# Attention and a linear-attention branch in one kernel: the four query chunks of a head group taken one after the other, with the order of the work written anew

## The chip, the cores and the metric

The kernel runs on one core of one Trainium2 chip. The metric is the device time of one execution in microseconds (us). The core has a matrix engine (PE), a vector engine (DVE), a scalar engine for activations (ACT), a general engine (POOL) and a queue for transfers (SP). They run side by side and wait for one another through semaphores.

## The reference, cut to what matters

The input x has 2048 tokens of 512 values. Two branches of 32 heads of 16 values each are computed from it and mixed by a gate per token.

```python
def _A_ref(x, wqkv, wo):                      # softmax attention
    q, k, v = ...                             # 32 heads of 16
    scores = jnp.einsum("bhqd,bhkd->bhqk", q, k) * (Dh ** -0.5)
    p = _softmax(scores, axis=-1)
    o = jnp.einsum("bhqk,bhkd->bhqd", p, v)
    return ... @ wo
def _B_ref(x, wqkv, w_phi, wo):               # linear attention
    phi_q = concat(softmax(q @ w_phi), softmax(-(q @ w_phi)))   # the same for k
    kv = einsum(phi_k, v); z = sum(phi_k)
    o = (phi_q @ kv) / (phi_q @ z + 1e-6)
    return ... @ wo
g = _sigmoid((x * gate_w).sum(-1, keepdims=True))
return g * a + (1 - g) * b
```

Branch A needs 32 x 2048 x 2048 exponentials, which is most of the work.

## The kernel before, in words

**Tiles of branch A.** The 2048 queries are cut into four chunks of 512 (`qc` 0 to 3), the 32 heads into four groups of eight (`cp` 0 to 3). A *step* is one pair (qc, cp). `ORDER` lists the 16 steps. Each step has two halves of four heads, so there are 32 half steps. A half step goes through the 16 tiles of 128 keys; one such tile for four heads is a *pack* (512 packs in all), and a pack has four *units*, one for each head: 128 keys by 512 queries, held as a 128x512 tile. There are 2048 units.

**Two ways for a unit.** Most units go through ACT: PE makes the scores in a ring of five PSUM banks (`_scores`, L1253), ACT takes the exponential of three and of two units in turn (`_exp`, L1304), and PE multiplies the result with the values (`_values`, L1378). Some packs are taken from ACT: `SHARES` says how many packs of each half step. Such a pack is a *batch* (`_vector_batch`): DVE copies each of its four score tiles out of PSUM with a scale (`v_bits`, L1155), and then four instructions over all four units (`v_line`, L1167) make four bit patterns, which read as bf16 numbers add up to the exponential. Bits of `POOLED` say which of the four lines of a batch run on POOL; the others run on DVE. PE then multiplies each pattern with the values, two of the four with values weighted by a constant. These weighted values lie in `VW` and are made on POOL by `v_scale` (L1131), four instructions each time `cp` differs from that of the step before.

**Projections.** Queries of a step are projected some 42 packs ahead (`_proj_q`, copied to `qraw`, moved by eight small transfers to `qT`). Keys and values are projected once for each group `cp` and each quarter j of the tokens (`_proj_k`, copied at L961; `_proj_v`, copied at L1041), and stay in `kT` and `V` to the end. Their due time is that of the group's first step plus `KAT + KSTEP*j` (values `VAT + VSTEP*j`), in packs. In the order of before each group is first met at step 0, 2, 4 and 6, so all keys and values are made in the first half.

**Normalising and output of A.** After each half step the sums are transposed, divided and scaled by the gate on DVE (`_norm`, `_normed`), and written to `onTA`, which has three buffers taken in turn by `qc`.

**Branch B.** Keys first (`_b_keys`, due at `K0 + SK*t` for token tile t), then queries in four blocks of four tiles (`_b_queries`, due at `Q0 + SQ*t`). Both go through `_b_soft`: a projection, a copy (L1548), a tree of maxima and differences on DVE, one exponential on ACT (L1585), a transposing transfer to `turns` (L1593), sums on PE and a scaling on DVE. Queries go on by a transposing transfer to `phiT` (L1671), to the product with the keys' sums, to `onB` (L1698), and by a transposing transfer to `onTB` (L1703). `onTB` has room for four token tiles, so a block's transfer waits until the block before has been read by the output.

**Output.** For each token tile eight matmuls, four from `onTB` (L1719) and four from `onTA` (L1763), then a copy on DVE (L1749) and a transfer out. `_out` puts a chunk's four tiles after its last step (`_done`), the last chunk's go through `_out_last` (L1791, L1801, L1804).

**The order.** The kernel writes out a fixed instruction order for each engine. `Plan.order` is a list scheduler that runs while the kernel is built: each operation has a cost, a due time (`prio`) and an earliest time (`rel`), in packs; it takes the operation that can start first, and among those the one that is due first. `NUDGE`, `HURRY`, `EASE`, `QEASE`, `LEASE` and `OEASE` are tables that shift single due times. Engines run their list in order, so one late operation holds all behind it. `PORT` names the operations which the scheduler never lets run on DVE and POOL at the same time: the lines, the scalings of `VW`, and the elementwise operations of branch B and the normalising among them; it writes a wait for that. When PE would have too little to do, it gets matmuls with zero weights (`_fill`, L1387).

Of the kernel before, what the change touches and what calls it, by code (L numbers as in the profile page):

```python
# [10 lines left out]
P = 128  # L11
# [58 lines left out]
class Plan:  # L70
# [10 lines left out]
    AHEAD, ENTER = 0.11, 0.011  # L81
# [310 lines left out]
class _Kernel:  # L392
# [6 lines left out]
    POOLED = (2, 15, 3, 10, 13, 12, 9, 14, 2, 6, 0, 7, 1, 13, 12, 3, 4, 11, 1, 1, 1, 13, 14, 0, 1, 0, 6, 10, 10, 2, 1, 3, 0, 1,  # L399
# [16 lines left out]
    OREL = 2  # L416
    ENDS = 10
    HURRY = (-10.7, 3.7, -1.9, -3.8, -1.4, 0.0, 0.0, 4.8, -2.6, -5.6, 17.9, 7.0, -7.0, 13.6, -1.6, 6.6, 2.3, 4.9, 15.5, 9.2,
# [5 lines left out]
    HASTE = 10  # L424
    QEASE = (0, 6.0, -7.0, 2.5, 3.8, 2.2, -6.3, -1.1, 0.2, -0.1, 6.2, -3.3, 0.0, 0.0, 0.4, -5.5)
    LEASE = (4.5, 6.9, -6.1, -1.6, 8.1, -2.7, 0, 0.0, 2.8, 1.7)
    OEASE = (0.3, 0, 0, 0, -0.6, 4.1, -0.7, 1.8, 5.0, 0, 3.4, 0, 0, 0, 0, 0)
    EASE = (14.0, -3.9, -11.6, 0.0, -2.6, 1.9, 2.0, 3.6, 4.6, -1.0, -0.8, -4.4, 6.4, 3.2, -1.7, 4.3, -1.2, -3.8, -1.2, 1.8,
# [5 lines left out]
    NUDGE = {  # L434
        'b_max': {1: 5.0, 2: 3.3, 3: -27.2, 4: 8.3, 6: -1.0, 7: 1.5, 8: -16.1, 10: -11.6, 13: 5.1, 14: -22.6, 16: -3.1,
# [5 lines left out]
        'b_mul': {1: -7.8, 4: 7.4, 5: -7.7, 7: -0.3, 8: 10.2, 9: 3.3, 10: 7.3},  # L441
        'b_ratio': {1: -4.3, 2: -18.2, 3: -0.7, 4: 2.1, 5: 5.9, 7: -0.2, 8: 18.9, 9: 3.5, 10: 7.2},
        'b_rec': {1: -6.3, 2: 3.4, 3: 5.3, 4: 23.1, 5: 0.9, 6: 14.6, 7: 0.9, 10: 1.4},
        'b_sum': {1: -4.9, 2: -2.5, 3: 1.1, 4: -8.4, 5: -1.9, 6: -4.7, 8: -18.1, 9: -18.6, 10: 3.4, 11: 2.3, 12: -30.0,
            13: -7.5, 14: -7.7, 15: 3.8, 18: 1.9, 19: 5.2, 20: -10.9, 21: 6.2, 23: -4.0, 24: -1.0, 25: -4.7, 26: 10.3,
            27: 9.6, 28: 2.4, 29: 9.6, 30: -23.7, 32: -0.3},
        'bn_den': {2: -10.7, 3: -2.5, 4: 5.5, 5: 4.0, 6: 9.9, 8: -11.3},
        'bn_mul': {2: -13.6, 3: 2.6, 4: -19.3, 5: -3.4, 6: 3.9, 7: -9.5, 8: -8.8, 9: 0.9, 11: -5.8, 12: 9.2, 13: 2.2,
            14: -0.5, 15: 3.7},
        'bn_rec': {1: 13.8, 2: -0.5, 4: -0.9},  # L450
# [5 lines left out]
        'bv_ev': {1: 24.2, 2: 11.4, 3: -6.4, 4: 3.4, 5: 1.7, 7: -6.7, 10: -8.6, 11: -23.4, 12: -3.9, 13: 4.1, 14: -4.1,  # L456
            15: -10.2},
        'den': {1: -23.3, 2: 16.1, 3: 5.2, 4: -4.6, 5: 9.8, 6: 8.6, 8: -20.2, 10: -3.7, 11: -10.3, 12: -3.5, 13: 5.0,
            14: -1.3, 16: -4.7, 18: 2.4, 19: 17.5, 20: 19.9, 21: -3.2, 23: -3.7, 24: -6.7, 25: -9.8, 26: -9.1, 29: -0.3,
            30: 10.3, 31: -0.4, 32: 6.9},  # L460
        'kproj': {1: 0.8, 3: 16.6, 4: 2.3, 5: -16.1, 6: 11.8, 9: -13.0, 10: 2.0, 11: 12.0, 12: 10.1, 13: -21.2, 14: -6.2,
# [808 lines left out]
    def _qk(self, a, b):  # L1270
# [582 lines left out]
```

## Time and profile before

| | |
|---|---|
| three timed runs | 779.84, 782.51, 783.31 us (median 782.51) |
| the profiled execution | 779.79 us, of which 778.0 us are the span of its instructions |
| ACT busy | 761.5 us of the span |
| PE, DVE, POOL busy | 746.7, 660.3, 337.3 us |
| batches taken from ACT | 110 of 512 packs (the sum of `SHARES`) |
| lines of these batches | 440, of them 160 on POOL |

An engine's busy time is the union of its instructions' times, so that instructions that overlap are not counted twice; the mean of one instruction is its whole duration. "Idle before" is the idle time of the engine in front of an instruction, with the instruction of the other engine that ended it. PE's busy time holds the zero matmuls too.

### The profile page before, as it was taken

The page shows a single profiled execution, that of the slowest core. Times are in us where ns is not written, and L with a number is a line of the kernel's source. Part 1 is how long each engine was busy: PE and PEld are TensorE (multiplying, and loading weights), DVE is VectorE, ACT ScalarE, POOL GpSimd, SP SyncE. Part 2 cuts the span into 40 slices and gives each one's busy share as a digit, 9 for nine tenths or more (in the row PEclk, how much of TensorE's full clock was granted, in tenths as well). Part 3 has the DMA queues.
Part 4 walks back from the last instruction along what each step waited for, and adds up shares of the span by engine and source line. Part 5 has one row for each costly group of instructions (what it writes and reads, how often), then busy time and mean ns, then how long its engine had stood idle before and what let it go on. Part 6 is the DMA issues. An engine that isn't in the chain of part 4 may idle for free.

```text
span 778.0 us, 20056 instructions
## 1 busy us (share of the span) xinstructions
PE 746.7 (96%) x8809; PEld 263.7 (34%) x8844; DVE 660.3 (85%) x1158; ACT 761.5 (98%) x658; POOL 337.3 (43%) x215
## 2 busy tenths in 40 slices
PE   8999999999999999999999999999999999999998
PEld 4333332333333333323333233322323333333345
DVE  5678887998889898888988898889897998888996
ACT  7999999999999999999999999999999999999997
POOL 4634254543432523554562423533435434354540
PEclk9999999999999999999999999999999999999999
DMA  9601110100304000003310033200024010331100
GB/s 240 198 5 35 28 30 7 29 8 2 63 1 63 1 2 8 2 1 63 69 22 28 3 59 64 37 21 5 5 43 75 2 22 15 62 56 29 28 3 31
DMA packets 82311, 28.44 MB, mean 37 GB/s; under 512 B 71984, under 2 KB 82224, under 8 KB 82224
## 3 DMA queue, kind: packets, MB, share of 16 engines
q1 hardware_dynamic: 81552, 26.97, 17.3%
q8 instruction: 69, 1.13, 0.6%
q10 hardware_dynamic: 672, 0.20, 0.1%
q14 instruction: 18, 0.15, 0.1%
HBM read 6.31 MB, written 2.10 MB: 11 GB/s over the span
## 4 chain that ended last, share of the span: by engine, by line
ACT 44%; PE 28%; DVE 19%; POOL 7%; issue 1%; DMA 1%; DVEq 0%
ACT ET L1304 43%; PE ps L1253 9%; PE ps L1378 7%; DVE blocks L1155 5%; DVE blocks L1167 5%; POOL blocks L1167 4%; PE ps L939 4%; PE ps L1387 3%; POOL over L1167 2%; DVE over L1167 2%; DVE over L1155 1%; DVE octs L1583 1%; ACT bq L1585 1%; PE ps L1035 1%; DMA turns<-bq 1%
## 5 line engine op out<-in xcount | busy, mean ns | idle before, releaser
L1304 ACT ACTIVATE ET<-ps 128x1536 bf16<-128x1536 f32 (+1 forms) x643 | 732.5, 1298 | 6.1 <-PE ps L1253 5.4
L1253 PE MATMUL ps<-qT,kT 32*128 32x512 bf16 (+2 forms) x2248 | 305.9, 364 | 12.1 <-ACT ET L1304 4.2
L1167 POOL TENSOR_SCALAR blocks<-blocks 128x2048 int16<-128x2048 f16 x85 | 161.3, 1897 | 167.7 <-DVE over L1167 64.6
L1155 DVE TENSOR_SCALAR blocks<-ps 128x512 f16<-128x512 f32 x316 | 207.2, 683 | 25.6 <-PE ps L1253 24.5
L1253 PEld LDWEIGHTS ps<-qT,kT 32*128 32x128 bf16 x2248 | 83.5, 91 | 248.7 <-ACT ET L1304 115.3
L1378 PE MATMUL ps<-ET,V 128*32 128x512 bf16 (+2 forms) x1772 | 146.3, 363 | 0.7 <-DVE over L1155 0.3
L1387 PE MATMUL ps<-kT,zero 128*32 128x512 bf16 (+1 forms) x1460 | 119.8, 384 | 0.0
L1167 DVE TENSOR_SCALAR blocks<-blocks 128x2048 int16<-128x2048 f16 x153 | 103.5, 687 | 11.8 <-POOL blocks L1167 6.2
L1155 DVE TENSOR_SCALAR over<-ps 128x512 f16<-128x512 f32 x124 | 81.6, 683 | 11.6 <-PE ps L1253 11.2
L1167 POOL TENSOR_SCALAR blocks<-over 128x2048 int16<-128x2048 f16 x27 | 51.2, 1897 | 91.5 <-DVE over L1167 31.5
L1167 POOL TENSOR_SCALAR over<-blocks 128x2048 int16<-128x2048 f16 x28 | 53.1, 1897 | 55.7 <-DVE blocks L1167 14.9
L1378 PE MATMUL ps<-blocks,VW 128*32 128x512 bf16 (+1 forms) x692 | 60.7, 365 | 1.7 <-DVE blocks L1167 1.0
L1378 PE MATMUL ps<-blocks,V 128*32 128x512 bf16 (+1 forms) x676 | 60.7, 368 | 1.6 <-DVE blocks L1167 0.6
L1378 PEld LDWEIGHTS ps<-ET,V 128*32 128x32 bf16 x1772 | 42.7, 96 | 48.6 <-issue 29.1
L1167 POOL TENSOR_SCALAR over<-over 128x2048 int16<-128x2048 f16 x20 | 37.9, 1897 | 42.2 <-DVE blocks L1167 22.3
L1131 POOL TENSOR_SCALAR VW<-V 128x544 bf16<-128x544 bf16 x40 | 25.7, 645 | 66.7 <-PE ps L1378 24.1
L1387 PEld LDWEIGHTS ps<-kT,zero 128*32 128x32 bf16 x1460 | 31.9, 94 | 53.8 <-issue 43.8
L939 PE MATMUL ps<-WB,xT 128*128 128x512 bf16 x169 | 45.8, 381 | 4.3 <-issue 2.3
L1167 DVE TENSOR_SCALAR blocks<-over 128x2048 int16<-128x2048 f16 x50 | 34.4, 688 | 5.4 <-PE ps L1253 2.8
L1167 DVE TENSOR_SCALAR over<-blocks 128x2048 int16<-128x2048 f16 x50 | 34.3, 687 | 5.0 <-POOL blocks L1167 3.5
L939 PE MATMUL ps<-xT,WA 128*128 128x512 bf16 (+1 forms) x124 | 35.7, 380 | 1.4 <-DVE blocks L1155 0.8
L1585 ACT ACTIVATE bq<-octs 128x4096 bf16<-128x4096 f16 (+1 forms) x10 | 29.8, 2979 | 0.0
(98 smaller groups left out, 533.6 us busy)
## 6 DMA issues: line engine op xcount, KB each, us to landing
qT<-qraw SPq DMA_DIRECT2D x120, 16.0 KB, 1.8
xn<-in_A_x_dram SPq DMA_DIRECT2D x3, 512.0 KB, 6.0
WB<-in_B_wqkv_dram SPq DMA_DIRECT2D x3, 512.0 KB, 5.2
out_dram<-WB SPq DMA_DIRECT2D x12, 128.0 KB, 1.7
WA<-in_A_wqkv_dram SPq DMA_DIRECT2D x3, 384.0 KB, 4.5
xn<-in_A_x_dram SPq DMA_DIRECT2D x2, 256.0 KB, 3.6
WoA<-in_A_wo_dram SPq DMA_DIRECT2D x1, 512.0 KB, 4.1
WoB<-in_B_wo_dram SPq DMA_DIRECT2D x1, 512.0 KB, 4.9
```

Of the source, the lines that this page charges most:

```text
L939: mm = op("PE", lambda e, c=c: e.matmul(self._bank(job)[:, 0:n], lhs(c), rhs(c), start=(c == 0), stop=(c == 3)), self.c_pe(n), reads=reads ...
L1035: ins = e.matmul(self._bank(job)[:, P * tt:P * tt + P], self.xT[:, 4 * j + tt, c], self.WA[:, 2, c, P * cp:P * cp + P], start=(c == 0), st ...
L1131: self.plan.op("POOL", lambda e, q=q: e.tensor_scalar(self.VW[:, q, 0:544].rearrange("p (t v) -> p t v", v=136), self.V[:, 4 * q:4 * q + 4 ...
L1155: parts.append(op("DVE", lambda e, j=j, job=job: e.tensor_scalar(x[:, j, :], self._bank(job), SCALE * LOG2E * 128, FLOOR, op0=ALU.mult, op ...
L1167: op("POOL" if pooled else "DVE", lambda e, tile=tile, line=line: e.tensor_scalar(flat(tile).bitcast(I16), flat(x), 1.0, line, op0=ALU.mul ...
L1253: ins = e.matmul(out[u][:, cols], self.kT[32 * i:32 * i + 32, cp, kt * TOK:(kt + 1) * TOK], self.qT[32 * i:32 * i + 32, s, q], start=True, ...
L1304: o = plan.op("ACT", lambda e: e.activation(self.ET[:, a % NS:a % NS + n, :], self.ps[:, a % NR:a % NR + n, :], ACT.Exp, scale=SCALE), sel ...
L1378: ins = e.matmul(self._bank(ot)[32 * i:32 * i + 32, to], values, tile[:, cols], start=first and j == 0, stop=ot.final[i] is op and j == le ...
L1387: ins = e.matmul(self._bank(ot)[32 * i:32 * i + 32, lo:QCH], self.zero[:], self.kT[:, 0, lo:QCH], start=False, stop=False, tile_position=( ...
L1583: return e.tensor_tensor(wide(signs(off_)[:, :, s_]), a, b, ALU.subtract)
L1585: made = [op("ACT", lambda e: e.activation(flat, off_, ACT.Exp), 0.03 + self.c_act(n), reads=b_half, name="b_exp", prio=due + 1, lat=0.53)]
```

## The change

The steps are taken in another order: all four chunks of group 0, then all four of group 1, and so on. With it:

- Keys and values of group `cp` are due from 96 (84) packs before the group's first step on, 24 packs apart, where it was 42 (36) and 12. As before, each is projected once.
- All four chunks are now finished in the last quarter, so `onTA` has four buffers. Room for that comes from `qraw` (one buffer for two), and from `wphi` and `iden`, which now share memory with `onB`. `phiT` lies over the first half of `kT` (groups 0 and 1), no longer over `WA`; its first transfer waits for the readers of these keys.
- The zero matmuls read `xT`, no longer `kT`.
- `v_scale` follows the change of group: at 4 of the 16 steps, where it was 10.
- Branch B is drawn out: keys due at 18 + 16t (was 18 + 9.5t), queries at 330 + 12t (was 216 + 17t).
- `SHARES` sums to 113 (was 110): by groups of eight half steps 28, 27, 34, 24, where it was 22, 29, 31, 28. Of the 452 lines 161 are marked for POOL (44, 34, 47, 36 by the same groups; before 43, 43, 40, 34).
- Every table of shifts is another one, and three constants of the scheduler (`AHEAD`, `OREL`, the latency of the transfer to `onTB`).

```diff
-    AHEAD, ENTER = 0.11, 0.011
+    AHEAD, ENTER = 0.07, 0.011
...
-    ORDER = ((0, 0), (1, 0), (0, 1), (1, 1), (0, 2), (1, 2), (0, 3), (1, 3),
-             (2, 0), (3, 0), (2, 1), (3, 1), (2, 2), (2, 3), (3, 2), (3, 3))
+    ORDER = tuple((qc, cp) for cp in range(4) for qc in range(4))
-    KAT, KSTEP, VAT, VSTEP = -42, 12, -36, 12
+    KAT, KSTEP, VAT, VSTEP = -96, 24, -84, 24
-    OREL = 2
+    OREL = 3
...
+        self.wphi = nc.alloc_sbuf_tensor_at("wphi", [P, 4, P], BF16, offset=onb_at)
+        self.iden = nc.alloc_sbuf_tensor_at("iden", [P, P], BF16, offset=onb_at + 1024)
+        self.qraw = sb("qraw", [P, 1, QCH], BF16)
+        self.onTA = sb("onTA", [P, 4, 4, QCH], BF16)
-        self.phiT = nc.alloc_sbuf_tensor_at("phiT", [P, 4, 8, TOK], BF16, offset=wa_at + 4 * D * 2)
+        self.phiT = nc.alloc_sbuf_tensor_at("phiT", [P, 4, 8, TOK], BF16, offset=kt_at)
...
-    SHARES = (1, 2, 3, 5, 2, 3, 4, 2, 3, 5, 3, 4, 3, 4, 3, 4, 4, 3, 4, 3, 4, 6, 3, 4, 3, 5, 3, 2, 4, 5, 3, 3)
+    SHARES = (2, 3, 3, 3, 4, 6, 2, 5, 2, 4, 3, 5, 3, 4, 2, 4, 5, 5, 4, 4, 3, 4, 3, 6, 1, 6, 1, 3, 3, 3, 3, 4)
...
-                e.matmul(self.ps[:, a % NR, :], self.kT[:, 0, 0:P], self.kT[:, 0, 0:QCH], start=True, stop=True)
+                e.matmul(self.ps[:, a % NR, :], self.xT[:, 1, 0], self.xT[:, 1].rearrange("p c q -> p (c q)"), start=True, stop=True)
...
-        dst, b_dst = self.onTA[:, qc % 3, g8 // 2, :], self.b_onTA[qc % 3][g8 // 2]
+        dst, b_dst = self.onTA[:, qc, g8 // 2, :], self.b_onTA[qc][g8 // 2]
...
-    K0, SK, Q0, SQ = 18.0, 9.5, 216.0, 17.0
+    K0, SK, Q0, SQ = 18.0, 16.0, 330.0, 12.0
...
+        if not self.b_early:
+            self.b_early = [*self.b_k0, *self.b_kT[0], *self.b_kT[1]]
+            for b in self.b_phiT:
+                b.readers = [r for x in self.b_early for r in x.readers]
...
-            reads=self.b_onB, writes=self.b_onTB[tt:tt + 2], prio=due + 2, lat=2.9)
+            reads=self.b_onB, writes=self.b_onTB[tt:tt + 2], prio=due + 2, lat=3.1)
```

More of the change, by code (lines that the diff above doesn't have):

```diff
@@ L678, in sb @@
             return t
-        self.iden = sb("iden", [P, P], BF16)
         self.mask = sb("mask", [P, 2], F32)
@@ L703, in _memory @@
         self.sides = sb("sides", [P, 2, 4], BF16)
+        kt_at = (at[0] + 63) // 64 * 64
         self.kT = sb("kT", [P, 4, S], BF16)
@@ L712, in _memory @@
         self.rB = sb("rB", [P, 2, H], F32)
+        onb_at = (at[0] + 63) // 64 * 64
         self.onB = sb("onB", [P, 2, D], BF16)
-        self.qraw = sb("qraw", [P, 2, QCH], BF16)
-        self.onTA = sb("onTA", [P, 3, 4, QCH], BF16)
+        self.wphi = nc.alloc_sbuf_tensor_at("wphi", [P, 4, P], BF16, offset=onb_at)
+        self.iden = nc.alloc_sbuf_tensor_at("iden", [P, P], BF16, offset=onb_at + 1024)
+        self.qraw = sb("qraw", [P, 1, QCH], BF16)
+        self.onTA = sb("onTA", [P, 4, 4, QCH], BF16)
         wt_at = (at[0] + 63) // 64 * 64
@@ L846, in _projections @@
         self.b_qraw = [B(), B()]
-        self.b_onTA = [[B() for _ in range(4)] for _ in range(3)]
+        self.b_onTA = [[B() for _ in range(4)] for _ in range(4)]
         self.b_T1 = [B(), B()]
@@ L1015, in _proj_q @@
         reads = [self.b_xT[qc], self.b_WA[0][cp > 0], self.b_mask]
-        raw = self.qraw[:, n % 2]
+        raw = self.qraw[:, 0]
         self._proj(lhs, rhs, reads, [lambda e, b: e.tensor_copy(raw, b)], self.c_dve(512), due, due - 10, "qproj",
-                   [self.b_qraw[n % 2]])
+                   [self.b_qraw[0]])
         parts = [lambda e, i=i, side=side: e.dma_start(
@@ L1021, in _proj_q @@
             raw[32 * i + 16 * side:32 * i + 16 * side + 16, :]) for side in range(2) for i in range(4)]
-        o = self.plan.op("SP", parts, 0.63 * len(parts), reads=[self.b_qraw[n % 2]], writes=[self.b_qT[s0]],
+        o = self.plan.op("SP", parts, 0.63 * len(parts), reads=[self.b_qraw[0]], writes=[self.b_qT[s0]],
                          deps=self.b_qT[s0 + 1].readers + [self.o_qzero], name=f"dma_q{n}", prio=due, lat=2.2)
@@ L1386, in _fill @@
         for i in range(4):
-            ins = e.matmul(self._bank(ot)[32 * i:32 * i + 32, lo:QCH], self.zero[:], self.kT[:, 0, lo:QCH], start=False,
+            ins = e.matmul(self._bank(ot)[32 * i:32 * i + 32, lo:QCH], self.zero[:], self.xT[:, 1].rearrange("p c q -> p (c q)")[:, lo:QCH], start=False,
                            stop=False, tile_position=(0, 32 * i), skip_group_check=True)
@@ L1458, in _branch_b @@
         self.b_phiT = [B() for _ in range(4)]
-        for b in self.b_phiT:
-            b.readers = [r for s in (1, 2) for b in self.b_WA[s] for r in b.readers]
+        self.b_early = []
         self.b_onB, self.b_rB = [B(), B()], B()
@@ L1468, in _branch_b @@
             b.readers = list(self.b_WT.readers)
+        for b in self.b_onB:
+            b.readers = self.b_wphi.readers + self.b_iden.readers
         self.linear = []
@@ L1743, in _out @@
             first[0].rel = due - 6
-            first[0].deps += [w for b in self.b_onTA[qc % 3] for w in b.writers]
+            first[0].deps += [w for b in self.b_onTA[qc] for w in b.writers]
             for o in first:
@@ L1753, in _tokens @@
     def _tokens(self, qc, pr, tt):
-        on = self.onTA[:, qc % 3, pr]
+        on = self.onTA[:, qc, pr]
         if qc == self.NQC - 1 and pr == 3:
@@ L1764, in mm @@
                                 self.WoA[:, pr, :], start=acquire is not None, stop=(pr == stop))
-            m = self.plan.op("PE", mm, self.c_pe(512), reads=[self.b_onTA[qc % 3][pr], self.b_WoA], deps=[m], name="outa",
+            m = self.plan.op("PE", mm, self.c_pe(512), reads=[self.b_onTA[qc][pr], self.b_WoA], deps=[m], name="outa",
                              prio=due, acquire=acquire)
```

111 lines of the change are left out of this document (52 added, 59 removed), and 340 rows, old and new, of tables (EASE, HURRY, NUDGE, POOLED).

## The prediction

> **What bounds the kernel now.** I read the page's busy times first, then the waits of ACT, then ACT's timeline at both ends.
>
> ```profile
> PE 746.7 (96%) x8809; PEld 263.7 (34%) x8844; DVE 660.3 (85%) x1158; ACT 761.5 (98%) x658; POOL 337.3 (43%) x215
> ACT 44%; PE 28%; DVE 19%; POOL 7%; issue 1%; DMA 1%; DVEq 0%
> ACT ET L1304 <- PE ps L1253: 5.4, 13, 0.9
> 7.35 33.34 ACT L1304 ACTIVATE ET<-ps 128x1536 bf16<-128x1536 f32 x29 [0.49 <-PE ps L1253]
> 729.17 43.05 ACT ET L1304 x38
> L1304 ACT ACTIVATE ET<-ps 128x1536 bf16<-128x1536 f32 (+1 forms) x643 | 732.5, 1298 | 6.1 <-PE ps L1253 5.4
> L1585 ACT ACTIVATE bq<-octs 128x4096 bf16<-128x4096 f16 x6 | 22.1, 3682 | 0.0
> L1585 ACT ACTIVATE bq<-octs 128x2048 bf16<-128x2048 f16 x4 | 7.7, 1924 | 0.0
> L1387 PE MATMUL ps<-kT,zero 128*32 128x512 bf16 (+1 forms) x1460 | 119.8, 384 | 0.0
> ```
>
> ACT is busy for 98% of the span. Its first exponential starts at 7.35 us and its last one ends at 729.17 + 43.05 = 772.22. Between the two it waits 13 times, for 5.4 us in all, each time for scores. PE's 96% is no second bound, since the zero matmuls of L1387 fill its gaps (1460 of them, last row). The span is therefore 7.35 us of start, ACT's work, 5.4 us of stalls, and 5.8 us of end. The chain names other engines for half of its length because ACT and its feeders run in step; what counts is how much ACT has to do and how often the feeders make it wait.
>
> **Term 1, exponentials.** `SHARES` goes from 110 to 113 packs, so three packs or 12 units leave ACT. There are 2048 - 440 = 1608 units now, in 643 instructions of 732.5 us: 0.4556 us a unit. The mean of 1298 ns is not used, since it counts the overlap of neighbours twice. 12 x 0.4556 = **-5.5 us**, and 1596 units should show as 639 instructions. Branch B's ten exponentials (22.1 + 7.7 us) stay.
>
> The number of projections does not change. Before, too, keys and values are projected once for each group; the change only moves them. So nothing is saved there, and the gain must come from Term 1, if DVE and POOL can carry the three batches.
>
> **Term 2, DVE.** A batch is four copies (L1155) and four lines (L1167). What one costs when instructions stand back to back is read from starts:
>
> ```profile
> 712.59 2.49 DVE L1167 TENSOR_SCALAR blocks<-blocks 128x2048 int16<-128x2048 f16 x4
> 714.99 0.69 DVE L1155 TENSOR_SCALAR blocks<-ps 128x512 f16<-128x512 f32 x1
> 715.59 0.69 DVE L1167 TENSOR_SCALAR blocks<-blocks 128x2048 int16<-128x2048 f16 x1
> ```
>
> Four lines take 714.99 - 712.59 = 2.40 us, and a copy 715.59 - 714.99 = 0.60: both cost 0.60 us, though one lasts 0.69. Three batches are 12 copies and 12 lines, of which 161 - 160 = 1 is POOL's: 23 x 0.60 = 13.8 us more for DVE. That makes 674 of a span of 772.5, or 87% for 85%. On the whole this fits. By quarter it is tighter. The quarters of the run (eight half steps each) end where the count of exponentials reaches 170, 328 and 483 of 643; the rows are all engines by quarter, then in the third quarter the copies and the lines alone on DVE, then three stretches in which DVE is fullest:
>
> ```profile
> 0.00:209.80 209.80, 201.57 (x2120) 75.14 (x2130) 168.84 (x313) 203.00 (x177) 96.73 (x69) 1.00 0.26 60
> 209.80:395.00 185.20, 178.55 (x2062) 60.79 (x2064) 161.72 (x277) 183.18 (x158) 82.27 (x48) 1.00 0.13 22
> 395.00:577.40 182.40, 176.04 (x1926) 56.10 (x1937) 158.50 (x268) 182.38 (x157) 72.38 (x43) 1.00 0.13 26
> 577.40:772.20 194.80, 187.52 (x2679) 69.84 (x2681) 168.44 (x294) 192.58 (x168) 85.97 (x56) 1.00 0.19 35
> 395.00:577.40 182.40, 74.59 (x114) 1.00 0.13 26
> 395.00:577.40 182.40, 51.83 (x78) 1.00 0.13 26
> 220.00:240.00 20.00, 19.54 (x207) 6.39 (x206) 19.47 (x35) 20.00 (x17) 3.79 (x2) 1.00 0.01 2
> 520.00:540.00 20.00, 19.43 (x215) 5.89 (x216) 19.31 (x33) 20.00 (x19) 7.59 (x4) 1.00 0.03 9
> 560.00:580.00 20.00, 19.17 (x218) 5.92 (x215) 19.69 (x36) 20.00 (x17) 3.80 (x2) 1.00 0.03 8
> ```
>
> In the third quarter DVE is now busy for 158.5 of 182.4 us. 114 copies and 78 lines are 192 x 0.60 = 115.2 of it; 43.3 are the rest. By the tables it should have been 31 x 4 = 124 copies and 124 - 40 = 84 lines, 208; so 16 instructions fell behind into the fourth quarter, and ACT was still busy for 182.38 of 182.40. After the change the quarter has 136 copies and 136 - 47 = 89 lines, 225. The rest of 43 I leave: eight copies of keys and values come in (group 3, due at packs 288 to 360), eight copies of output go out, and the second block of queries of branch B is due at 370, near the quarter's end, so that about as much of it lies inside as before. With the same 16 left behind it is 209 x 0.60 + 43 = 168 us. ACT needs 376 x 0.4556 + 2 x 3.68 = 178.7 us. That asks 94% of DVE, where the fullest quarter now is 161.72 of 185.20, 87%. The first gains 47 instructions (88 + 45 by the tables to 112 + 68; 28 us) and gives up eight projection copies (5 us) and four of the twelve tiles of branch B in it, which brings it to about nine tenths. The second stays; the fourth falls from 112 + 78 and what was left behind to 96 + 60, with eight output copies and one more block of branch B added.
>
> Bounds of this term: the three stretches hold DVE at 97 to 98% for 20 us and ACT at 20.00 of 20.00, so the crowding can cost nothing. If DVE cannot go beyond 87% over a whole quarter, the quarter takes 168/0.873 = 193 us, 14 more. I take **+0.7**, near the stretches, because the work left behind has an empty fourth quarter to go to.
>
> **Term 3, POOL and the shared operations.**
>
> ```profile
> L1131 POOL TENSOR_SCALAR VW<-V 128x544 bf16<-128x544 bf16 x40 | 25.7, 645 | 66.7 <-PE ps L1378 24.1
>   DVE blocks L1167: 1.8, 6
>   DVE over L1167: 0.6, 2
> L1167 POOL TENSOR_SCALAR blocks<-blocks 128x2048 int16<-128x2048 f16 x85 | 161.3, 1897 | 167.7 <-DVE over L1167 64.6
> ```
>
> Of 40 scalings of `VW` 24 go: 24 x 0.645 = 15.5 us of POOL, against one line more of 1.9. POOL is idle more than half of the time, so its own time is free. But the code lets no line run on DVE beside them; DVE waited 1.8 + 0.6 = 2.4 us for all 40 (the two indented rows), so 1.4 us of DVE time come back. The Trainium skill (SBUF — State Buffer, Who interferes with whom) says that GpSimd and a VectorE instruction in a two-port mode hold the shared ports for the whole instruction and that the other one blocks fully; by that alone the 24 would give DVE back up to 15.5 us. The row of waits has a sixth of that, as DVE had PSUM copies to do meanwhile, and the row decides here. On ACT I take **-0.3**, between 0 and the 1.4.
>
> **Term 4, what stands ahead of scores on PE.** PE runs its list in order, and ACT's larger stalls show what was in front:
>
> ```profile
> 251.50 1.45 ACT L1304 ACTIVATE ET<-ps 128x1536 bf16<-128x1536 f32 x1 [0.88 <-PE ps L1253]
> 250.58 0.56 PE L1599 MATMUL ps<-sides,turns 128*128 128x8 bf16 x16 [0.65 <-DMA turns<-bq]
> 721.67 6.89 ACT L1304 ACTIVATE ET<-ps 128x1024 bf16<-128x1024 f32 x6 [0.80 <-PE ps L1253]
> 729.17 16.84 ACT L1304 ACTIVATE ET<-ps 128x1024 bf16<-128x1024 f32 x15 [0.61 <-PE ps L1253]
> 719.85 0.81 PE L1719 MATMUL ps<-WoB,onTB 128*128 128x512 bf16 x3 [0.16 <-issue]
> 720.50 0.81 PE L1763 MATMUL ps<-WoA,onTA 128*128 128x512 bf16 x3
> ```
>
> At 251.5 PE sat in front of branch B's sums until the transfer to `turns` had landed, behind a projection of keys; at 721.7 and 729.2 two output tiles had just gone through. In the order of before eight of the twelve tiles of chunks 0 to 2 go out in the third quarter, where ACT has no such stall, and four in the fourth, with 0.80 + 0.61 = 1.41. Afterwards all twelve go out in the fourth. Between no cost and three times 1.41 (+2.8) I take **+0.7**: the quarter has only 24 batches in PE's list. Drawing out branch B and the projections parts what met at 251.5; I take **-0.9** for that, between -0.9 and +0.9. The moved query projections keep their eight transfers each, and `qraw` as one buffer has a step of 48 us between uses, so SP's order costs nothing.
>
> **Term 5, the end.** `onTB` must be read by tiles 8 to 11 before it can be filled for the last four.
>
> ```profile
> L1719 PE MATMUL ps<-WoB,onTB x13: 379/379/390, 698.9 to 727.6; 128*128 128x512 bf16 x13
> L1703 SPq DMA_TRANSPOSE onTB<-onB x8: 1190/1266/2202, 629.3 to 729.2; - x8
> DMA to landing us min/median/max: 2.4/2.5/4.2
> L1791 PE MATMUL ps<-WoB,onTB x18: 272/379/389, 761.5 to 774.8; 128*128 128x512 bf16 x10, 128*128 128x256 bf16 x8
> ```
>
> Now the last of these reads is at 727.6, the last transfer is issued at 729.2, and the first use is at 761.5: some 30 us of cover. Afterwards tile 11 is due at pack 505, not before 499, which is about 19 us before ACT's last exponential ends (12.8 packs, 80% of them on ACT, at 1.82 us). Transfer and landing take 1.3 + 1.3 + 2.5 = 5, and the third of the last tiles, the first that needs this pair, may start at pack 507, some 7 us before the end. About 6 us of cover are left. With the longest landing (4.2) it still holds: **0**, with +1.7 as the upper bound.
>
> **The sum.** -5.5 + 0.7 - 0.3 + 0.7 - 0.9 = -5.3. The profiled execution took 779.79 us for its span of 778.0; it would take 774.5. The three timed runs are 779.84, 782.51 and 783.31, so it stands at their lower end, 2.7 below the median. Put on the median, 782.5 - 5.3 gives the forecast, **777.2 us**. About 0.5%, or 3.9 us, is what a measurement can tell from no change, so this is faster by little more than that.
>
> **The rivals.**
>
> *DVE full in the third quarter* (slower). ACT's scores queue on PE behind products that wait for lines. For it speaks the demand of 94% against a fullest quarter of 87%; against it the 20-us stretches at 98% without a stall. At 87% it costs 14: 782.5 - 5.3 - 0.7 + 14 = 790.5. It outweighs Term 1 from a limit below about 168/(178.7 + 5.5) = 91% on.
>
> *The crowded last quarter* (no change). Output tiles cost 2.8 in place of 0.7 and the end 1.7: 782.5 - 5.3 + 2.1 + 1.7 = 781.0. For it speaks that 16 output tiles, two blocks of branch B and the normalising of all chunks' last steps meet there; against it that this quarter has the fewest batches. A part of the first rival's stall ends here too.
>
> *The stalls go* (more gain). The 5.4 us of waiting on ACT fall to 1, as fewer things collide when projections and keys are spread: 782.5 - 5.5 - 4.4 = 772.6. For it speaks that 2.3 of the 5.4 us are the three stalls shown, all of them meetings of two neighbours; against it that new neighbours bring new collisions.
>
> *The change does not do what it says*: 113 batches would be fewer if the count were otherwise; then 643 exponentials would remain. The tables leave no room for that.
>
> **How the numbers follow.** The forecast's case, 774 to 779.5, has a chance of 0.47; the stalls go, 0.16; the crowded quarter, 0.20; DVE full, 0.17. A tenth of the forecast's case ends within 0.5%. Faster by over 0.5%: 0.47 x 0.9 + 0.16 = 0.58. Within it: 0.05 + 0.20 = 0.25, of which 0.02 go to slower. Slower: 0.17 + 0.02 = 0.19; within: 0.23. The range for 8 in 10 reaches from 771 (the third rival's better half) to 787 (the first rival's milder half).
>
> **What would show it.** Right: 639 exponentials, about 727 us of them; ACT waiting 4 to 7 us between the first and the last; 16 scalings of `VW`; DVE at 92% or more in the third quarter and ACT still full there; the last transfer to `onTB` landing before PE asks for it. Wrong: stalls of ACT behind L1378 waiting for L1167 in the third quarter (the first rival), stalls behind L1719 and L1763 after 620 us (the second), or an end longer than 5.8 us.

## The result

The changed kernel takes 779.34 us (median of 20 executions, 778.28 to 780.54), the kernel before 779.88 (20 executions, 779.26 to 783.31). The ratio is 0.9984, with a 95% interval of 0.9976 to 0.9992: a gain of 0.5 us by the medians and of 1.2 by the ratio, and inside the 0.5% that were called no change. The profiled execution takes 778.32 us with a span of 776.5, against 779.79 and 778.0: 1.5 us less, where the prediction's sum says 5.3. In some executions of nearly every kernel the recorded matrix clock falls to half for a few microseconds, and one such stretch makes them 0.8 to 1.9 us longer (1.1 in the changed kernel); where medians of executions at full clock are given beside the others, that is why.

The page of the changed kernel: its engines, the chain's shares, and the groups of exponentials and scalings:

```profile
PE 750.1 (97%) x8852; PEld 263.3 (34%) x8852; DVE 672.4 (87%) x1181; ACT 756.1 (97%) x654; POOL 324.4 (42%) x192
ACT 48%; PE 31%; DVE 15%; POOL 5%; DMA 2%; issue 1%; DVEq 0%; POOLq 0%
L1313 ACT ACTIVATE ET<-ps 128x1536 bf16<-128x1536 f32 x639 | 727.2, 1296 | 6.7 <-PE ps L1262 6.0
L1140 POOL TENSOR_SCALAR VW<-V 128x544 bf16<-128x544 bf16 x16 | 10.4, 647 | 42.2 <-DVE blocks L1176 13.5
```

639 exponentials for 643, and 5.3 us less of them: ACT has less to do, as planned. The span did not follow. ACT's waits (total, times, longest) and the last lines of its timeline say where it went:

```profile
ACT ET L1313 <- PE ps L1262: 6.0, 14, 0.8
ACT xT L1818 <- PE ps L1805: 5.8, 1, 5.8
```

```profile
760.39 4.63 ACT L1313 ACTIVATE ET<-ps 128x1024 bf16<-128x1024 f32 x4 [0.19 <-PE ps L1262]
765.84 1.51 ACT L1313 ACTIVATE ET<-ps 128x1024 bf16<-128x1024 f32 x2 [0.83 <-PE ps L1262]
773.19 0.39 ACT L1818 ACTIVATE xT<-ps 128x256 bf16<-128x256 f32 x1 [5.84 <-PE ps L1805]
```

The stalls between the exponentials are about what they were (6.0 us for 5.4). The last exponential ends at 765.84 + 1.51 = 767.35 instead of 772.21, but then ACT waits 5.84 us in front of the last copy, where before it waited 2.4 (the next row). From the last exponential to the end it is 776.5 - 767.35 = 9.15 us, before 5.8. The 3.4 us lost there and 0.6 of stalls take 4.0 of the 5.3 that the exponentials gained. With a first exponential 0.1 us earlier that leaves 1.4 us, and 1.5 were measured.

```profile
ACT xT L1804 <- PE ps L1791: 2.4, 1, 2.4
```

PE's timeline at the end shows what the end is made of, first in the kernel before, from its last exponential on:

```profile
772.26 0.41 PE L1378 MATMUL ps<-ET,V 128*32 128x128 bf16 x16 [0.17 <-ACT ET L1304]
772.83 0.81 PE L1791 MATMUL ps<-WoB,onTB 128*128 128x512 bf16 x3 [0.16 <-issue]
773.48 1.14 PE L1791 MATMUL ps<-WoA,onTA 128*128 128x512 bf16 x5
774.45 0.60 PE L1791 MATMUL ps<-WoB,onTB 128*128 128x256 bf16 x4
774.89 0.60 PE L1791 MATMUL ps<-WoA,onTA 128*128 128x256 bf16 x4
```

and after the change, from shortly before it:

```profile
763.58 1.03 PE L1733 MATMUL ps<-WoB,onTB 128*128 128x512 bf16 x4
764.44 1.03 PE L1777 MATMUL ps<-WoA,onTA 128*128 128x512 bf16 x4
765.40 0.42 PE L1262 MATMUL ps<-qT,kT 32*128 32x128 bf16 x12
...
767.58 0.41 PE L1387 MATMUL ps<-over,VW 128*32 128x128 bf16 x16
...
770.05 0.40 PE L1387 MATMUL ps<-blocks,VW 128*32 128x128 bf16 x16
770.38 1.04 PE L1805 MATMUL ps<-WoB,onTB 128*128 128x512 bf16 x4
...
773.43 0.60 PE L1805 MATMUL ps<-WoA,onTA 128*128 128x256 bf16 x4
```

Tile 11's eight output matmuls stand in front of the last scores (before, they ran at 727.1 to 728.8). Behind the last exponential come 192 products, from 767.58 to 770.4, and the last two tiles of the output. Before, 16 products and 16 output matmuls were left at that point. In rows, from each kernel's last exponential on (stretch, length to the query's end, then busy time of PE, PEld, DVE, ACT and POOL, the granted clock, the DMA share and GB/s), the kernel before:

```profile
772.21:785.00 12.79, 3.06 (x32) 1.81 (x33) 2.77 (x9) 0.39 (x2) 0.00 (x0) 1.00 0.07 22
```

and after the change:

```profile
767.35:785.00 17.65, 6.68 (x218) 4.96 (x216) 5.16 (x15) 0.39 (x2) 0.00 (x0) 1.00 0.17 44
```

PE's work behind the last exponential grew by 3.6 us, and the end by 3.4. The quarters (the second to the fourth, same columns):

```profile
208.00:399.00 191.00, 183.82 (x2087) 62.33 (x2083) 173.91 (x293) 189.00 (x163) 74.20 (x43) 1.00 0.08 15
399.00:577.00 178.00, 173.56 (x1963) 56.57 (x1960) 162.48 (x278) 177.89 (x156) 82.37 (x44) 1.00 0.10 19
577.00:767.40 190.40, 184.49 (x2451) 69.12 (x2448) 157.29 (x277) 188.85 (x161) 74.16 (x41) 1.00 0.30 52
```

DVE is at 91% in the third quarter (162.48 of 178.00) and ACT at 177.89 of 178.00: the place that the prediction feared most costs nothing.

### The profile page after: what moved, and what is told of

It is laid out like the page before. It is cut to its first block, busy times and chain, and to the rows that moved or that the text cites. A ratio compares the mean times of both kernels' runs of the same rounds, so it can differ in the third digit from the quotient of the medians.

```text
span 776.5 us, 20099 instructions
## 1 busy us (share of the span) xinstructions
PE 750.1 (97%) x8852; PEld 263.3 (34%) x8852; DVE 672.4 (87%) x1181; ACT 756.1 (97%) x654; POOL 324.4 (42%) x192
## 4 chain that ended last, share of the span: by engine, by line
ACT 48%; PE 31%; DVE 15%; POOL 5%; DMA 2%; issue 1%; DVEq 0%; POOLq 0%
ACT ET L1313 46%; PE ps L1262 10%; PE ps L1387 8%; DVE blocks L1164 4%; PE ps L948 4%; PE ps L1396 3%; POOL blocks L1176 3%; DVE blocks L1176 2%; ACT bq L1595 2%; DVE over L1164 2%; DMA phiT<-bq 2%; DVE over L1176 1%; POOL over L1176 1%; PE ps L1805 1%; PE ps L1044 1%
## 5 line engine op out<-in xcount | busy, mean ns | idle before, releaser
L1313 ACT ACTIVATE ET<-ps 128x1536 bf16<-128x1536 f32 x639 | 727.2, 1296 | 6.7 <-PE ps L1262 6.0
L1176 POOL TENSOR_SCALAR blocks<-blocks 128x2048 int16<-128x2048 f16 x89 | 169.1, 1900 | 208.7 <-DVE blocks L1176 69.8
L1164 DVE TENSOR_SCALAR blocks<-ps 128x512 f16<-128x512 f32 x324 | 211.3, 682 | 23.1 <-PE ps L1262 21.5
L1396 PE MATMUL ps<-xT,zero 128*32 128x512 bf16 (+1 forms) x1396 | 114.5, 383 | 0.0
L1164 DVE TENSOR_SCALAR over<-ps 128x512 f16<-128x512 f32 x128 | 84.2, 682 | 10.3 <-PE ps L1262 9.6
L1387 PE MATMUL ps<-blocks,VW 128*32 128x512 bf16 (+1 forms) x720 | 63.2, 362 | 0.9 <-issue 0.4
L1176 POOL TENSOR_SCALAR over<-over 128x2048 int16<-128x2048 f16 x17 | 32.3, 1901 | 52.8 <-DVE blocks L1176 35.4
L948 PE MATMUL ps<-WB,xT 128*128 128x512 bf16 x192 | 52.1, 382 | 1.8 <-DVE over L1164 1.2
L1396 PEld LDWEIGHTS ps<-xT,zero 128*32 128x32 bf16 x1396 | 30.3, 94 | 48.3 <-issue 39.4
L1140 POOL TENSOR_SCALAR VW<-V 128x544 bf16<-128x544 bf16 x16 | 10.4, 647 | 42.2 <-DVE blocks L1176 13.5
```

Source lines behind the costliest of these rows:

```text
L948: mm = op("PE", lambda e, c=c: e.matmul(self._bank(job)[:, 0:n], lhs(c), rhs(c), start=(c == 0), stop=(c == 3)), self.c_pe(n), reads=reads ...
L1140: self.plan.op("POOL", lambda e, q=q: e.tensor_scalar(self.VW[:, q, 0:544].rearrange("p (t v) -> p t v", v=136), self.V[:, 4 * q:4 * q + 4 ...
L1164: parts.append(op("DVE", lambda e, j=j, job=job: e.tensor_scalar(x[:, j, :], self._bank(job), SCALE * LOG2E * 128, FLOOR, op0=ALU.mult, op ...
L1176: op("POOL" if pooled else "DVE", lambda e, tile=tile, line=line: e.tensor_scalar(flat(tile).bitcast(I16), flat(x), 1.0, line, op0=ALU.mul ...
L1313: o = plan.op("ACT", lambda e: e.activation(self.ET[:, a % NS:a % NS + n, :], self.ps[:, a % NR:a % NR + n, :], ACT.Exp, scale=SCALE), sel ...
L1387: ins = e.matmul(self._bank(ot)[32 * i:32 * i + 32, to], values, tile[:, cols], start=first and j == 0, stop=ot.final[i] is op and j == le ...
```

## Experiments

**A ledger for all of them.** Theory ACT: a batch is worth its 1.82 us of exponentials wherever it stands, and what is missing was lost to stalls. Theory END: PE and DVE are full at the end, so what ACT saves in the last half step comes back as waiting. Each row is one profiled execution; "end" is the span less the end of the last exponential. (The profile of sought_111 has a long stretch at half clock; its end is 5.6 us as well.)

The runs come from several series, and the kernel before, run again in each, has at full clock 780.14 us (beside last_step_110, last_step_112, tile11_small and batch509_quarter), 779.62 (before_last4, batch509_dve, scalings_small, gap_filled), 779.95 (last_step_111, sought_111, sought_113) and 780.15 (sought_111_filled). In the series of the changed kernel its clocks are not on record. So a difference of some 0.5 us between the median of an experiment and that of the changed kernel shows nothing by itself; the argument goes by the rows of the profiles and by comparisons within a series.

| kernel | batches | order | exponentials | ACT's waits for scores | last exponential ends | PE busy behind it | end | span |
|---|---|---|---|---|---|---|---|---|
| before | 110 | old | 732.5 | 5.4 | 772.21 | 3.06 | 5.8 | 778.0 |
| before_last4 | 111 | old | 730.9 | 5.6 | 771.25 | 8.51 | 11.7 | 782.9 |
| last_step_110 | 110 | new | 732.7 | 5.2 | 771.88 | 1.78 | 4.9 | 776.8 |
| last_step_111 | 111 | new | 731.0 | 6.0, and 2.0 behind products | 772.77 | 2.24 | 4.8 | 777.6 |
| last_step_112 | 112 | new | 729.0 | 6.2 | 769.19 | 6.14 | 9.7 | 778.9 |
| after | 113 | new | 727.2 | 6.0 | 767.35 | 6.68 | 9.15 | 776.5 |
| sought_113 | 113 | sought again | 727.2 | 5.2 | 766.78 | 7.39 | 11.1 | 777.9 |
| sought_111_filled | 111 | sought again | 731.1 | 6.2 | 771.45 | 2.66 | 5.6 | 777.0 |

The stalls between the first and the last exponential are 5.2 to 6.2 us in every kernel, with the 2.0 of last_step_111 beside them. The end moves between 4.8 and 11.7 us, and PE's work left behind the last exponential moves with it.

**How many batches the last half step holds.** Only the last entry of `SHARES` differs, and with it what the scheduler makes of the order:

```diff
-    SHARES = (2, 3, ..., 3, 3, 3, 3, 4)
+    SHARES = (2, 3, ..., 3, 3, 3, 3, 1)     # last_step_110; 2: last_step_111; 3: last_step_112
```

> The changed kernel with 1 batch in the last half step in place of 4 (110 batches in all, as before the change); the rest of the program as it is. Theory ACT (each batch taken from ACT is worth its 1.82 us wherever it stands): +5.5 us against the changed kernel, about +4 against the kernel before. Theory END (from about 760 us on PE has more work than time, so ACT's saving in the last half step only waits for PE at the end): between -1 and +0.5 us against the changed kernel; ACT's last exponential ends 4 to 5 us later and the time behind it falls from 9.2 us to about 5.5.

> The changed kernel with two batches fewer in its last half step (the last entry of SHARES 4 becomes 2: 111 batches), its order made from the same tables. All runs so far agree in one ledger: the time between ScalarE's first and last exp is that of the exps plus 5 to 7 us of waiting, whatever was changed, and what differs is the end, read as ScalarE's wait in front of its last copy (2.4 us before, 5.8 after, 2.2 with 110 batches, 7.0 with 112, 9.0 in the kernel before with one batch more). Theory END: two batches fewer cost 3.6 us of exps and give the end back up to 3.6 us: 778.3 to 780.5 by where the last products are put. Theory ACT: +3.6 us against the changed kernel, 782.5.

> The changed kernel with 3 batches in the last half step in place of 4 (112 in all): the batch of pack 509 goes back to ACT. Theory ACT: +1.8 us against the changed kernel. Theory END: within 1 us of it, as PE gets rid of four products and four scores of some 1.5 us in the stretch where it is full.

With 110 batches the median is 778.93 (778.25 to 779.60), 0.9979 of the kernel before (0.9967 to 0.9991): no slower than the changed kernel with its 113. ACT forecast 5.5 us more. ACT's lines of this run:

```profile
L1313 ACT ACTIVATE ET<-ps 128x1536 bf16<-128x1536 f32 (+1 forms) x643 | 732.7, 1296 | 6.0 <-PE ps L1262 5.2
ACT xT L1818 <- PE ps L1805: 2.2, 1, 2.2
```

As many exponentials as before the change, and an end 0.9 us shorter: the new order is worth about 1.2 us of span, and the three batches, which save 5.5 us of exponentials, are worth 0.3 us of span beside it (776.5 for 776.8) and nothing by the ratios. With 111 the median is 780.00, ratio 0.9994 (0.9983 to 1.0005); a single stall of 2.00 us behind products in the last half step, beside its 6.0 for scores, makes it dearer. With 112 it is 782.02, ratio 1.0012 (1.0000 to 1.0024), more than with 110, 111 or 113. Here the end has a picture of its own, in PE's timeline:

```profile
768.57 1.04 PE L1805 MATMUL ps<-WoB,onTB 128*128 128x512 bf16 x4 [0.48 <-DMA onTB<-onB]
...
771.71 0.41 PE L1387 MATMUL ps<-blocks,VW 128*32 128x128 bf16 x16
771.95 1.51 PE L1387 MATMUL ps<-ET,V 128*32 128x128 bf16 x96
775.87 0.39 PE L1805 MATMUL ps<-WoA,onTA 128*128 128x256 bf16 x2
```

The output matmuls that could go were put in front, 112 products wait behind them, and then the normalising on DVE of two groups, one after the other, stands between the products and the last two matmuls. So neither theory holds alone. By the ledger (776.8, 777.6, 778.9, 776.5) the first batch more costs 0.8 us of span, the second 1.3, and the third brings 2.4: what a batch there is worth is no constant, and is set by how the rest of the last half step is laid out.

**One batch more in the old order.**

```diff
-    SHARES = (1, 2, ..., 2, 4, 5, 3, 3)
+    SHARES = (1, 2, ..., 2, 4, 5, 3, 4)
```

> The kernel before with one batch more in its last half step (the last entry of SHARES 3 becomes 4: 111 batches), its order otherwise made from the same tables. Theory ACT (a batch takes a pack off ScalarE, 1.82 us, wherever it stands): -1.8 us against the kernel before. Theory END (the last half step has no room left on TensorE and VectorE, a batch there only comes later): between 0 and +3 us.

784.35 us (783.60 to 785.55), ratio 1.0048 (1.0029 to 1.0067): some 3.8 us slower than the kernel before, and 4.9 in the profiled span, which is beyond END's bound of 3. The exponentials fell by 1.6 us as they should, and ACT's last wait rose from 2.4 to 9.0:

```profile
ACT xT L1804 <- PE ps L1791: 9.0, 1, 9.0
```

```profile
775.65 0.69 DVE L1167 TENSOR_SCALAR blocks<-over 128x2048 int16<-128x2048 f16 x1 [2.27 <-PE ps L1378]
```

A line of the last batch waited 2.27 us for products to free its buffer, and those stood on PE behind the output (16 of them only at 777.20). Here a batch added without seeking the order again did harm; that part of the change is not an ornament.

**Work taken away at the end, order kept.**

```diff
 # tile11_small: tile 11's eight output matmuls write 4 of 512 columns
 # batch509_quarter, in _values:
+            if p == 509 and j < 3:
+                continue
 # batch509_dve: this, and the lines of the same batch that run on DVE:
+            lo = 384 if p == 509 and not pooled else 0
```

> The changed kernel in the same order, with the eight output matmuls of token tile 11 cut from 512 columns to 4 (its output is left out): about 1.3 us less PE work at 763.6 us. Theory ACT: only ACT's stall of 0.83 us at 765.8 goes, at most -0.8 us, and the time behind ACT's last exponential stays at 9 us. Theory END: -1.3 to -2.1 us, some of it behind the last exponential.

> The changed kernel in the same order, with three quarters of the products of the batch of pack 509 left out (48 of 64 matmuls, some 0.7 us of PE after ACT's last exponential). Theory ACT: no change. Theory END: -0.5 to -0.7 us, all of it behind the last exponential.

> The changed kernel in its own order; of the batch for pack 509, the last one, 48 of 64 products are left out as in the run batch509_quarter, and now VectorE's lines for that batch write a quarter of their columns too (the two at 768.49 and 769.33 us in the profile take some 0.2 us in place of 0.69). Theory DVE-END (behind the last exp VectorE's two late lines and TensorE's products end within 0.3 us of each other, so that cutting only the products gained nothing, PE having waited 0.32 us for the second line): with both cut the end comes 0.6 to 1.0 us earlier than in the changed kernel at the same clock, 777.9 to 778.3 against 778.9. Theory TRANSFER-END (the last transfer to onTB, issued at 765.9 us and 3.6 to 4.4 us under way, holds the last output matmuls at about 770): no more than 0.3 us, 778.6 to 778.9.

tile11_small (the output of tile 11 is left out): median 779.62, ratio 0.9982 (0.9966 to 0.9997). In its profile ACT runs from 753.67 to 767.82 us without a stall (its stretch at half clock lies ahead of that), where the changed kernel has 0.19 and 0.83, and waits longer in front of its last copy:

```profile
ACT xT L1820 <- PE ps L1807: 6.4, 1, 6.4
```

So of 1.02 us of stalls some 0.6 came back at the end (6.4 for 5.84), and 0.4 is left. Its four executions at full clock have a median of 778.45, the changed kernel's 13 have 778.90: 0.45 us came of 1.6 us of PE. Set against the kernel before of its own series (778.45/780.14 = 0.9978) it could be nearer 1 us, still less than END had said. That is my error in reading END: work in front of the last exponential costs only what ACT waits there, and part of that comes back.

batch509_quarter (most products of the last batch are left out): median 779.38, ratio 0.9976 (0.9962 to 0.9990); 778.75 at full clock (five executions). Its end is 9.0 us, hardly less than 9.15. The products that went had not been last alone, as PE now waited for DVE:

```profile
771.15 0.24 PE L1389 MATMUL ps<-blocks,VW 128*32 128x128 bf16 x4 [0.32 <-DVE blocks L1176]
```

With the lines cut too, PE goes from the products into the output without that wait, and ACT waits 5.17 us in front of its last copy, not 5.84:

```profile
770.69 0.23 PE L1391 MATMUL ps<-blocks,VW 128*32 128x128 bf16 x4
770.85 1.04 PE L1809 MATMUL ps<-WoB,onTB 128*128 128x512 bf16 x4
```

```profile
773.66 0.38 ACT L1822 ACTIVATE xT<-ps 128x256 bf16<-128x256 f32 x1 [5.17 <-PE ps L1809]
```

That wait shrank by 0.67 us, which is the work taken from PE there (6.00 us behind the last exponential for 6.68), and the end from 9.15 to 8.5. The median is 778.64, ratio 0.9972 (0.9962 to 0.9982), and 778.54 at full clock (ten executions): 0.4 us less than the changed kernel, between the two theories' numbers, though the two medians come from different series. In this profile the rest was lost ahead of the last exponential, where the waits are 6.9 us. So PE and DVE end together behind the last exponential, and it takes both to shorten the end. The transfer that fills `onTB` did not hold PE in these runs; in last_step_112 it did, for the 0.48 us shown.

**The order at the end sought anew.** The tables (`NUDGE`, `HURRY`, `EASE`, `QEASE`, `LEASE`, `OEASE`, `POOLED`) were altered at random for the last fifth of the run, and an alteration was kept when the plan that the scheduler writes ended no later with it. `SHARES` stays at 111 and at 113.

> As last_step_111, with the tables that set the order in the last fifth of the run (nudges, eases, hurries, which lines GpSimd takes) sought anew for 111 batches. Theory ORDER (the end is long because of where products and output tiles were put, not because 111 batches can't be carried): ScalarE's wait in front of the last copy 2.2 to 3.5 us, the last exp at 768 to 770, 776 to 777.5 us in all, and so 1.5 to 3 us less than the changed kernel. Theory FULL (TensorE's and VectorE's work in the last 25 us sets the end in any order): 778.3 or more.

> The changed kernel with all its 113 batches, the same tables sought anew for the last fifth of the run. Theory ORDER: the end comes back here too, 776 to 777.5 us. Theory FULL: with four batches in the last half step no order shortens the end, ScalarE's last wait stays at 5 to 7 us, 778.3 to 779.

sought_111: median 778.70, ratio 0.9981 (0.9966 to 0.9995), and 778.38 at full clock (seven executions), where last_step_111 with the same batches has 779.57 (five): 1.2 us from the order alone. ORDER is right about the end (5.6 us; ACT waits 2.9 in front of its last copy). It missed the 1.5 to 3 us against the changed kernel: that is 0.5 at full clock, from different series, and the time lies in FULL's range. sought_113: median 780.78, ratio 1.0003 (0.9990 to 1.0015), and 779.77 at full clock; its span is 1.4 us longer than that of the kernel it started from. Its last line on ACT:

```profile
775.31 0.38 ACT L1818 ACTIVATE xT<-ps 128x256 bf16<-128x256 f32 x1 [8.53 <-PE ps L1805]
```

With four batches in the last half step the end is long in all three orders that have them (9.15, 11.1, and 11.7 in the old one); with three it is 5.8 (before) or 9.7; with one or two 4.8 to 5.6. So with four no order here had room, as FULL says, and with three it hangs on the order. That another search would find a short end for 113 isn't excluded.

**Scalings of `VW`.** In the kernel before, 24 of the 40 scalings write 8 columns instead of 544, and the rest of `VW` keeps what it had.

```diff
+            w = 136 if n < 8 else 2
-            ... self.VW[:, q, 0:544] ... cp, 0:136], WEIGHT
+            ... [:, :, 0:w] ... cp, 0:w], WEIGHT
```

> The kernel before in its own order, with 24 of its 40 scalings on GpSimd (line 1131, 0.65 us each, those from the eighth step on) cut from 544 columns to 8, which is the number of scalings that the change takes away. The prediction's third term says -0.3 us (0 to -1.4) from 15.6 us of GpSimd spared; a rule by which a VectorE operation waits for the whole of a GpSimd operation beside it would make up to -15 us of it.

Median 780.55, ratio 0.9997 (0.9985 to 1.0010). At full clock its five executions have 778.86, the kernel before in the same series 779.62 (16 executions): -0.8 us, in the middle of the term's bounds. (Over all executions the ratio shows nothing, as 7 of the 12 had a stretch at half clock.) A scaling cut to 8 columns still takes 0.205 us, where it took 0.645, so 10.6 us of POOL went and not the 15.6 expected. The lines' waits for `VW` fell from 2.4 to 0.6 us.

**The stretch at half clock.** In the profile of tile11_small the clock (third column from the end) falls behind a wait for the last transfer to `phiT`:

```profile
747.53 0.26 PE L1697 MATMUL ps<-kvbd,phiT 128*128 128x4 bf16 x4 [0.80 <-DMA phiT<-bq]
```

```profile
748.00:750.00 2.00, 2.00 (x73) 1.56 (x64) 1.53 (x6) 1.83 (x2) 0.00 (x0) 1.00 0.58 155
750.00:753.60 3.60, 3.60 (x114) 2.51 (x109) 2.14 (x4) 2.90 (x3) 0.00 (x0) 0.53 0.24 48
753.60:756.00 2.40, 2.40 (x104) 1.95 (x104) 2.27 (x7) 2.33 (x3) 0.00 (x0) 0.99 0.22 44
```

Two kernels put zero matmuls there: twelve behind the filler of 745.92 in the changed kernel (the edit shown), and sixteen behind a group of scores in sought_111:

```diff
-        for i in range(4):
+        for i in list(range(4)) * (4 if self.fills == 343 else 1):
```

> The changed kernel in its own order with 12 zero matmuls more (3 times the 4 of line 1396, 0.64 us of PE by the row of 745.92 us, 0.40 for the first four and some 0.21 for every further four), put right behind the four at 745.92, in front of the wait for the last transfer to phiT. In the profile of the changed kernel PE waited there 0.49 us and the granted clock stayed at 1.0; in the profiles of the two kernels that differ from it only after 760 us PE waited 0.80 and 0.86 us at the same place, and 3 us later the clock was at half for 3.3 us. Theory GAP (the idle stretch of about 0.8 us before that transfer is what sets off the half clock): no execution with a mean clock of 0.998 from this place, a median of 778.9 (the changed kernel's executions at clock 1.0) and a narrower spread, -0.4 us against the changed kernel's median. Theory CHANCE (the clock drops for a reason that the kernel does not set): as before 7 in 20 executions at 0.998, median 779.3 to 779.5.

> The kernel of the run sought_111 with 16 zero matmuls more (4 times four, 384 columns; about 0.16 us of TensorE for every four) behind the scores at 752.18 us of its profile, in front of the wait for the last transfer to phiT, where TensorE waited 0.71 us and the clock then stood at half from about 753.6 to 760.2 us. 5 of 12 executions of sought_111 had two such stretches (mean clock 0.996, 781.0 us), 7 none (778.4). Theory GAP: nearly all executions at clock 1.0, a median of 778.4 (778.0 to 778.8), which is 0.9 us less than the changed kernel's median and 1.5 to 2 less than the kernel before. Theory CHANCE: again some 5 in 12 at 0.996 and a median of 778.7 or more.

gap_filled: median 778.94 (778.59 to 779.51), ratio 0.9976 (0.9966 to 0.9986). PE's wait is down to 0.22:

```profile
747.20 0.26 PE L1698 MATMUL ps<-kvbd,phiT 128*128 128x4 bf16 x4 [0.22 <-DMA phiT<-bq]
```

One of 12 executions had a lower mean clock, of the changed kernel 7 of 20. But batch509_dve, which has the changed kernel's order at this place and no zero matmuls added, had 2 of 12 in the same series. So gap_filled shows nothing about what they do.

sought_111_filled: median 779.09 (778.45 to 779.61), ratio 0.9969 (0.9956 to 0.9982), all 12 executions at full clock, where 5 of 12 were below it without the zero matmuls. In its profile PE still sits idle for 0.37 us at that place, where it was 0.71. The 778.4 expected were missed. The kernel before was slower in this series too: 780.15 at full clock, 779.95 in that of sought_111. Beside it the zero matmuls cost some 0.5 us at full clock (779.09/780.15 = 0.9986, 778.38/779.95 = 0.9980), and the spread is 1.2 us instead of 3.7. The kernel before had a lower clock in 10 of 17 executions of this series and in 12 of 29 of the other, so the series itself did not keep the clock up.

GAP fits this pair, from two series, and is not shown. Nor does the length of the wait say when the clock falls: with 110 and 111 batches PE waited 0.75 and 0.89 us at the same transfer in the profiled executions, and the clock stayed whole there. And it falls without such a wait. In scalings_small it is at half from about 262 us on, behind two waits of PE for DVE and none for a transfer in the 8 us before (the last row has the same columns as above):

```profile
259.56 0.38 PE L1254 MATMUL ps<-qT,kT 32*128 32x512 bf16 x1 [0.31 <-DVE VB L1532]
260.24 0.37 PE L1254 MATMUL ps<-qT,kT 32*128 32x512 bf16 x1 [0.30 <-DVE blocks L1156]
```

```profile
262.20:266.00 3.80, 3.80 (x21) 0.80 (x20) 3.02 (x6) 2.93 (x3) 1.90 (x1) 0.56 0.00 0
```

What sets such a stretch off stays open.

sought_111_filled has the lowest ratio of all. Its interval overlaps the changed kernel's, and the two were not run in one series, so that it beats the kernel before is shown, and that it beats the changed one is not.

## Why the prediction was right in its number and wrong in its sum

The 779.34 lie in the range and in the forecast's case (774 to 779.5). That is luck with the base: the forecast was put on 782.51, the median of three, and 20 executions have 779.88. On these the same sum gives 774.6, 4.8 us below the result; 5.3 us of gain were forecast, and 0.5 to 1.5 came. On the profiled execution the sum said 774.5, and it is 778.32.

- **Term 1, -5.5: right.** 639 exponentials and 5.3 us less of them.
- **Term 2, +0.7: 0.** DVE at 91% in the third quarter instead of the 94% forecast (and of the 92% named as a sign), and ACT full there: 177.89 of 178.00 us. 124 copies and 77 lines lay in it, 201 for the 209 forecast, as the second quarter took some of the batches' work ahead (114 and 83, by the tables 108 and 74). The rival of a full DVE is refuted; the 87% which it went by was no limit.
- **Term 3, -0.3: in its bounds.** The lines wait 0.9 us for `VW` (before 2.4):

```profile
  DVE over L1176: 0.5, 2
  DVE blocks L1176: 0.4, 2
```

  Cutting 24 scalings short in the kernel before gave -0.8 by itself. By the rule of the Trainium skill (SBUF — State Buffer, Who interferes with whom) up to 15.5 us could have come in the changed kernel and 10.6 in that run, as an estimate; neither shows it. The code keeps lines off DVE while scalings run, so the rule itself is not put to the test here.
- **Term 4, +0.7 - 0.9: about +0.6.** The sum of the two is off by 0.8, and neither part came as forecast. The three stalls at 251.5, 721.7 and 729.2 are gone, and ACT has others, 0.83 at 104.83 and 0.83 at 765.84, the latter behind tile 11. In the last quarter, where the twelve tiles go out, the stalls fell from 2.2 to 1.4 us instead of growing by 0.7; in the first half, where 0.9 should have gone, they grew from 3.2 to 4.6. The rival by which the stalls go is refuted: new neighbours met.
- **Term 5, 0 (at most +1.7): +3.4, the step that failed.** Two errors. Tile 11 was put 19 us before the last exponential's end, from its due time; its matmuls ran at 763.58, 3.8 us before it. And the end was asked only whether one transfer would land in time, which it did; PE's and DVE's own work in it was taken as given. It had grown from 3.06 to 6.68 us on PE. What should have been asked of Term 1 was when the last three batches' products and the output could run if ACT ended 5 us earlier.

The crowded last quarter was the rival nearest to what happened (781.0, no change): its end cost 3.4 rather than 1.7, its tiles next to nothing as stalls. "An end longer than 5.8 us" was named as what would prove the forecast wrong, and it came.

## What to carry to other kernels

Work taken off the fullest engine near the end pays only if the others can end earlier as well: list what each of them has left behind the last instruction of that engine, and cost that tail as a term of its own. An order planned by hand-tuned shifts belongs to its exact load; one batch more or less moved the end by several microseconds either way, so a single count tells nothing of the worth of a batch. Take the base from enough executions, and know what makes them differ, before forecasting a gain of half a per cent.

## What the runs showed of the hardware

A matrix engine that counts as 96% busy can still lose its clock: behind a wait of 0.80 us for a transfer, followed by matmuls of 4 columns, the granted clock was at 0.53 from 750.0 to 753.6, and in sought_111, behind a wait of 0.71 us, it was at 0.50 from 754 to 760:

```profile
754.00:760.00 6.00, 5.92 (x67) 2.61 (x66) 1.66 (x4) 3.57 (x4) 0.00 (x0) 0.50 0.26 46
```

In scalings_small waits of 0.31 and 0.30 us for DVE stood ahead of such a stretch, and in last_step_111 a wait of 0.89 us had none behind it. Executions of the changed kernel with a mean clock of 0.998, which is one such stretch (3.4 us at half clock take 0.002 from the mean of 778 us), took 780.0 us, those without 778.9; four with 0.996, which is two, took 781.54 in tile11_small against 778.45.

The Trainium skill (TensorE: Matmul & The Clock Gate, HAM oscillation — how this bites in real kernels) gives as the rule that no idle gap of TensorE should exceed about 3.4 us. The waits here were a quarter of that or less, so by these runs keeping under that length was not enough.

In tile11_small 3.6 us at 0.53 are as much as 3.4 us at half clock, and in scalings_small 3.8 us at 0.56 are 3.3. That agrees with the window of about 3.4 us that the Trainium skill names (TensorE: Matmul & The Clock Gate, Part 1: The HAM clock gate), which by that part runs freely. A free-running window would fit the wait of 0.89 us without a loss; no run here shows the window itself.
